# A gated mix of attention and a long convolution: operand layout, load sizes, a fourth buffer and a re-planned order

## The chip, the cores and the metric

The kernel runs on one core of a Trainium2 chip. The metric is the time of one execution on the device in microseconds, where lower is better. Three executions of the kernel before took 659.38, 667.66 and 668.18 us, so the median is 667.66 us. One further execution was profiled.

A core has engines that run side by side and synchronise by semaphores. TensorE (PE in the profile) multiplies matrices: a weight load (PEld) puts one operand into the array, and a matmul streams the other past it into PSUM. VectorE (DVE) and ScalarE (ACT) work element by element. GpSimd (POOL) makes constants here. SyncE (SP) issues nearly all transfers (DMA). Each engine takes its instructions strictly in the order written.

## What is computed

The inputs are one sequence `x` of 2048 positions with 448 channels, and the parameters of two branches. In short:

```python
g = sigmoid((x * gate_w).sum(-1, keepdims=True))
# a: 16 query heads of 28 channels, one key and one value head
q = x @ wq; k = x @ wk; v = x @ wv
p = softmax(q k^T * 28**-0.5)              # per head, 2048 x 2048
a = (p @ v) @ wo
# b: one causal convolution of length 2048 per channel
dt = exp(log_dt)
K[d, l] = Re(sum_n C[d,n] * exp(dt[d] * A[d,n] * l) * dt[d] * B[d,n])   # 256 complex n
b[:, d] = causal_convolution(x[:, d], K[d]) + x[:, d] * Dskip[d]
return g * a + (1 - g) * b
```

## The kernel before

**Attention.** `prep_x` transposes `x` into `xT` (channels on partitions) with TensorE and copies the result out of PSUM, half with ScalarE (L490) and half with VectorE (L492). It then makes keys (L498), values and the gate (L514). `qproj` (L649 to L661) makes the queries of four heads for 512 positions. `main` walks through 1024 tiles of scores, 128 keys by 512 queries each, in sets of three and two tiles by turns: the scores (L973, four heads in four row strips of the array), one exponential per set on ScalarE (L986), and, two sets later, the product with the values (L995, four heads in four column strips). Sixteen times an accumulator is finished; `norm` (L895 to L904) then moves the denominators through DRAM with nine transfers. `outp` multiplies with `wo` and `fold` adds the result into `O`.

**Convolution.** For each group of 32 channels VectorE builds tables of powers (`masters`, then `tables`, L744 to L781) in `tab`, and from them TensorE makes the kernel's values (`kgen`, L799), 16 channels per call, which go to the DRAM scratch `KP`. From there `tload` brings four channels as a Toeplitz operand of 1 MB into one of three slots of `T` (L824). `conv` (L841) multiplies it with `U`, a copy of `x` cut into pieces of 64 positions: for each slot there are 8 steps, each of them four matmuls, one per channel, side by side in four column strips. The weights are a column of `U` with one element every 448 (896 bytes), 32, 30, and so on down to 18 of them; the moving operand is 128 elements of `T` with one in four. A second product (L861) and an addition (L869) put the result into `O`.

**Where things lie.** Early data share memory with later data: `x` is staged in `tab`, the six parameter arrays in `O`, their products in `T`, `tmp` and `tab`, `wq` in `mbf`, and `wk` in `rho`. `consts` clears or fills buffers, some with long memsets on GpSimd: `Wq` with 2048 elements per partition, `Wo` with 1792, the second half of `U` with 7168. `prep_params` later clears `O` with 7168 (L632).

**What sets the order.** `Prog` collects the operations with their reads, writes, an assumed duration and a priority `pr` (a low number goes first). `schedule` is a planner at build time: it simulates the engines with the assumed durations and always takes the operation that can start earliest, among equals the one with the lowest `pr`. Scores have 0, values 0.5, kgen 1.7, the convolution 4. The order that results is fixed, and the semaphore waits are worked out from it (`emit`). A transfer is assumed to cost its issuing queue 60 ns, then a time for its bytes on one shared DMA resource, then 2200 ns (`DMA_NS`). The semaphore latency and extra slack are constants too. PSUM bank `psX` is shared by several steps under a lock.

Of the kernel before, what the change touches and what calls it, by code (L numbers as in the profile page):

```python
# [11 lines left out]
P = 128  # L12
# [18 lines left out]
NTR = 3  # L31
# [25 lines left out]
class Op:  # L57
    __slots__ = ("i", "eng", "fn", "ns", "lat", "deps", "pr", "lock", "unlock", "slot", "ndma",
                 "count", "vc", "end", "comm")


class Prog:
# [44 lines left out]
    def dma(self, pairs, desc, slot, rd=(), wr=(), pr=0, eng="sp", slow=False):  # L107
# [6 lines left out]
        o.slot, o.ndma = slot, len(pairs)  # L114
# [6 lines left out]
    def schedule(self):  # L121
# [19 lines left out]
        while done < n:  # L141
# [155 lines left out]
class Kernel:  # L297
# [25 lines left out]
    def alloc(self):  # L323
# [25 lines left out]
        self.U = sb("U", 32 * D, BF)  # L349
# [3 lines left out]
        self.rho = sb("rho", 32 * 64, BF)  # L353
        self.tmp = sb("tmp", 2 * 16 * EW, BF)
# [16 lines left out]
    def consts(self):  # L371
        pg = self.pg
        V = lambda b, off, n: b.v(0, P, off, [[1, n]])
        pm = lambda ap, val, ns, key, pr=0: pg.op("pool", lambda e: e.memset(ap, val), ns, wr=key, pr=pr)
        pm(V(self.ident, 0, P), 1.0, 200, ["id"])
# [3 lines left out]
        sm = self.small  # L379
        pm(V(self.Wq, 0, NT * 512), 0.0, 1500, ["Wq"])  # L380
        pg.op("dve", lambda e: e.tensor_reduce(V(sm, 0, 1), self.ident.v(0, P, 28, [[32, 4]]), AX.X, ALU.max),
              100, rd=["id"], wr=["s0"])
        pg.op("dve", lambda e: e.memset(V(sm, 1, 1), 0.5 * math.pi), 60, wr=["hpi"])
        pg.op("dve", lambda e: e.memset(V(self.Wk, 0, NT * P), 0.0), 300, wr=["Wk"])
        pm(V(self.Wm, 0, P), 0.0, 100, ["Wm"], 1)
        for hb in range(4):
            pm(self.Wm.v(32 * hb, 28, 32 * hb + 28, [[1, 1]]), -1.0, 60, ["Wm"], 1)
        pg.op("dve", lambda e: e.memset(self.vaug.v(0, P, 28, [[32, 16]]), 1.0), 80, wr=["va"])
        pg.op("dve", lambda e: e.memset(self.vaug.v(0, P, 29, [[32, 16], [1, 3]]), 0.0), 80, wr=["va"])
# [11 lines left out]
        pg.op("dve", lambda e: e.memset(V(self.kstg, 0, 256), 0.0), 100, wr=[("kst", 0)], pr=3)  # L401
        pm(V(self.skt, 0, D // 4), 0.0, 100, ["skt"], 4)
        pm(V(self.Wo, 0, NT * D), 0.0, 1500, ["Wo"], 4)
        pm(V(self.U, 16 * D, 16 * D), 0.0, 6000, ["U"], 5)

    def loads(self):
# [7 lines left out]
        raw = self.O  # L414
# [662 lines left out]
```

## Time and profile before

| what | value |
|---|---|
| median of three runs | 667.66 us (659.38 to 668.18) |
| the profiled execution's own time | 664.46 us |
| its span, first to last instruction | 662.7 us |
| mean granted TensorE clock | 0.828 |
| TensorE matmul busy | 553.9 us, 84% of the span |
| ScalarE busy | 498.3 us, 75% |
| VectorE busy | 475.7 us, 72% |
| GpSimd busy | 19.3 us, 3% |
| first exponential (L986) starts | 30.95 us |
| moved by transfers | 133.46 MB, mean 201 GB/s |

A row of a group reads: line, engine, operation, what it writes `<-` what it reads, shape, `x` count, then the busy time in us, the mean duration of one in ns, and the idle time just before these instructions with what ended it. A row of waits reads: engine, line and tile that waited, `<-` the engine and line that released it, total us, times, longest. A row of a timeline gives the start in us, the duration in us, the engine and the line; neighbouring instructions of one line are merged with their count, so a merged duration includes the run-out of the last one. Ends of matmuls are modelled, and a matmul that waits inside the array counts as busy.

### The profile page before, as it was taken

How to read it: one execution, taken by the hardware profiler on the slowest of the kernel's cores; microseconds unless marked ns; L12 is line 12 of the kernel's file. 1: busy time of each engine (PE TensorE's matmuls, PEld its weight loads, DVE VectorE, ACT ScalarE, POOL GpSimd, SP SyncE). 2: the span in 40 equal slices, each digit the busy share in tenths (PEclk: the TensorE clock that was granted, in tenths of full speed). 3: DMA queues.
4: the chain of work that ended last, by engine and by line, in shares of the span. 5: the costliest groups of instructions: out<-in, count | busy, mean ns of one | idle time of the engine just before them, and what ended most of it. 6: DMA issues, size and time to landing. Idle time of an engine off the chain costs nothing.

```text
span 662.7 us, 18405 instructions
## 1 busy us (share of the span) xinstructions
PE 553.9 (84%) x8234; PEld 269.0 (41%) x8234; DVE 475.7 (72%) x1045; ACT 498.3 (75%) x427; POOL 19.3 (3%) x24
## 2 busy tenths in 40 slices
PE   3787688999698988897889888988999987877775
PEld 2422132546354544453446345544554433311112
DVE  6679999898979999889797889989997221110002
ACT  3578778788778886886886787877888886779891
POOL 8003000000000000000000000000000000000000
PEclk9955557989899998899798998988988996855556
DMA  9630018787857678578778786878479669530000
GB/s 189 155 81 0 5 26 281 246 320 212 325 194 270 210 277 310 206 239 286 280 244 286 257 279 227 301 253 305 129 266 315 195 208 324 207 100 1 17 1 28
DMA packets 41262, 133.46 MB, mean 201 GB/s; under 512 B 10352, under 2 KB 24928, under 8 KB 26848
## 3 DMA queue, kind: packets, MB, share of 16 engines
q1 hardware_dynamic: 41184, 132.30, 59.9%
q8 instruction: 64, 1.05, 0.6%
q14 instruction: 14, 0.11, 0.0%
HBM read 128.31 MB, written 3.85 MB: 199 GB/s over the span
## 4 chain that ended last, share of the span: by engine, by line
PE 37%; DMA 29%; DVE 17%; ACT 12%; SPq 3%; issue 1%; DVEq 0%
DMA T<-KP_scratch 18%; ACT expT L986 12%; PE psS L973 9%; PE psS L841 8%; PE psX L799 6%; PE psB L995 6%; DMA denT<-acc 5%; SPq L111 3%; PE psX L649 2%; DVE tab L760 2%; DMA R_scratch<-denT 2%; DVE tmp L761 2%; DMA rdenB<-R_scratch 2%; DVE qT L661 1%; PE psX L878 1%; DVE acc L895 1%
## 5 line engine op out<-in xcount | busy, mean ns | idle before, releaser
L986 ACT ACTIVATE expT<-psS 128x1536 bf16<-128x1536 f32 (+1 forms) x410 | 483.5, 1255 | 134.4 <-PE psB L995 84.8
L973 PE MATMUL psS<-qT,kT 29*128 29x512 bf16 x1024 | 189.4, 458 | 43.2 <-ACT expT L986 42.1
L841 PE MATMUL psS<-T,U 128*32 128x128 bf16 (+7 forms) x3584 | 156.8, 307 | 31.7 <-DMA T<-KP_scratch 28.1
L841 PEld LDWEIGHTS psS<-T,U 128*32 128x32 bf16 (+7 forms) x3584 | 107.7, 155 | 77.8 <-DMA T<-KP_scratch 37.1
L995 PE MATMUL psB<-expT,vaug 128*32 128x512 bf16 x1024 | 111.7, 464 | 1.7 <-DVE acc L895 1.7
L973 PEld LDWEIGHTS psS<-qT,kT 29*128 29x128 bf16 x1024 | 40.5, 94 | 159.2 <-ACT expT L986 108.9
L799 PE MATMUL psX<-tab 128*32 128x64 bf16 x1792 | 78.7, 330 | 3.5 <-DVE kstg L812 1.7
L760 DVE TENSOR_TENSOR tab<-tab,mbf 128x4096 bf16<-128x4096 bf16 (+4 forms) x70 | 69.6, 995 | 0.0
L761 DVE TENSOR_TENSOR tmp<-tab,mbf 128x256 bf16<-128x256 bf16 (+4 forms) x70 | 69.2, 989 | 0.0
L799 PEld LDWEIGHTS psX<-tab 128*32 128x32 bf16 x1792 | 62.3, 155 | 16.3 <-issue 6.9
L995 PEld LDWEIGHTS psB<-expT,vaug 128*32 128x32 bf16 x1024 | 22.8, 97 | 64.0 <-issue 59.2
L895 DVE COPY acc<-psB 128x512 f32<-128x512 f32 x16 | 11.1, 692 | 44.8 <-PE psB L995 44.7
L763 DVE TENSOR_TENSOR tab<-tab,tmp 128x128 bf16<-128x128 bf16 (+4 forms) x70 | 39.9, 569 | 0.0
L850 DVE TENSOR_TENSOR cst<-psS,omq 128x512 bf16<-128x512 f32 x28 | 19.2, 686 | 28.5 <-PE psS L841 28.3
L765 DVE TENSOR_TENSOR tab<-tab,tmp 128x128 bf16<-128x128 bf16 (+4 forms) x70 | 39.7, 567 | 0.0
L776 DVE TENSOR_TENSOR tab<-tab,rho 128x4096 bf16<-128x4096 bf16 x14 | 32.0, 2288 | 0.0
L649 PE MATMUL psX<-xT,Wq 112*128 112x512 bf16 x64 | 22.5, 451 | 5.8 <-DVE Wq L440 5.8
L684 DVE TENSOR_TENSOR msq<-mst 128x256 f32<-128x256 f32 x63 | 27.1, 430 | 0.0
L904 DVE TENSOR_TENSOR onT<-acc,rdenB 128x512 bf16<-128x512 f32 x15 | 10.5, 702 | 22.8 <-DMA rdenB<-R_scratch 22.8
L772 DVE TENSOR_TENSOR rho<-rho,mbf 128x64 bf16<-128x64 bf16 (+4 forms) x70 | 25.4, 363 | 0.0
L900 DVE RECIPROCAL denT<-denT 128x16 f32<-128x16 f32 x15 | 3.8, 254 | 23.4 <-DMA denT<-acc 23.4
L869 DVE TENSOR_TENSOR O<-O,psX 128x256 bf16<-128x256 bf16 x28 | 11.6, 416 | 12.4 <-PE psX L861 12.3
(109 smaller groups left out, 351.0 us busy)
## 6 DMA issues: line engine op xcount, KB each, us to landing
T<-KP_scratch SPq DMA_DIRECT2D x112, 1024.0 KB, 7.2
rdenB<-R_scratch SPq DMA_DIRECT2D x60, 64.0 KB, 2.2
tab<-in_A_x_dram SPq DMA_DIRECT2D x4, 448.0 KB, 9.4
U<-in_A_x_dram SPq DMA_DIRECT2D x16, 112.0 KB, 3.0
KP_scratch<-kstg SPq DMA_DIRECT2D x28, 64.0 KB
out_dram<-O SPq DMA_DIRECT2D x3, 448.0 KB, 3.8
denT<-acc SPq DMA_DIRECT2D x60, 2.0 KB, 2.7
U<-in_A_x_dram SPq DMA_DIRECT2D x16, 56.0 KB, 2.2
```

Source lines behind the costliest of these rows:

```text
L649: pg.op("pe", lambda e, T=T: e.matmul(px, self.Wq.v(0, DT, T * 512 + g * 128, [[1, 128]]), self.xT.v(0, DT, T * S + 512 * qc, [[1, 512]]), ...
L684: pg.op("dve", lambda e, k=k: e.tensor_tensor(msq.v(0, P, 0, [[BW, 2], [1, BW]]), both(k - 1), both(k - 1), ALU.mult), el(2 * BW), rd=keys ...
L760: vo(lambda e, dst=dst, src=src, mr=mr: e.tensor_tensor(dst, src, mr, ALU.mult), 2 * n, done + mk(lv), [kr, ki])
L761: vo(lambda e, src=src, mi=mi, w=w: e.tensor_tensor(tmp.v(0, P, 0, [[w * EW, 2], [EW, w], [1, EW]]), src, mi, ALU.mult), 2 * n, done + mk( ...
L763: vo(lambda e, do=do, n=n: e.tensor_tensor(tab.v(0, P, do, [[1, n]]), tab.v(0, P, do, [[1, n]]), tmp.v(0, P, n, [[1, n]]), ALU.subtract), ...
L765: vo(lambda e, do=do, n=n: e.tensor_tensor(tab.v(0, P, do + BLK, [[1, n]]), tab.v(0, P, do + BLK, [[1, n]]), tmp.v(0, P, 0, [[1, n]]), ALU ...
L776: vo(lambda e: e.tensor_tensor(tab.v(0, P, FM, [[64, 2], [EW, 32], [1, 64]]), tab.v(0, P, lo + 31 * EW, [[BLK, 2], [-EW, 32], [1, 64]]), r ...
L799: r = e.matmul(self.psX.v(32 * g, 32, 64 * jj, [[1, 64]]), tab.v(0, P, lo + comp * BLK + 64 + o, [[EW, 32]]), tab.v(0, P, fo, [[mo - fo, 2 ...
L841: r = e.matmul(ps.v(32 * j, 32 - 2 * n, po + 128 * k, [[1, 128]]), self.U.v(0, P, 2 * n * D + 4 * gi + j, [[D, 32 - 2 * n]]), self.T.v(0, ...
L973: r = e.matmul(self.psS.v(0, P, 512 * (bo + k), [[1, 512]]), kT.v(32 * h, DH + 1, 128 * kt, [[1, 128]]), qT.v(32 * h, DH + 1, 512 * (i % 2 ...
L986: pg.op("act", lambda e: e.activation(expT.v(0, P, 512 * es, [[1, n]]), self.psS.v(0, P, 512 * bo, [[1, n]]), AF.Exp, scale=SQ), 130 + n / ...
L995: r = e.matmul(self.psB.v(32 * h, 32, 0, [[1, 512]]), vaug.v(0, P, 32 * kt, [[1, 32]]), expT.v(0, P, 512 * (t % 10), [[1, 512]]), start=(k ...
```

## The change

- `U` is stored as 448 channels times 32 pieces instead of 32 times 448, so the weights of a convolution step lie side by side. The loads can no longer write that order directly. They go to two staging halves in `tab` (behind the staged `x`), which VectorE clears first, and 16 copies on GpSimd reorder them into `U`.
- `T` gets a fourth slot. To make room, `rho` shares memory with `tmp`, `tmp` is halved, and the last doubling step of a table uses the `Fm` area of `tab` for its product. The parameter arrays are staged in `T`, their products in `T` and `mbf`.
- `x`, the projection weights and the parameters are loaded in rows of up to 3584 bytes, with four neighbouring positions or channels on one partition. The steps that read them undo the permutation by their strides (L490, L492 and the transposes). Three weight loads and `log_dt` are issued from ScalarE's queue.
- The clearing of `Wq` (now only its gaps), `Wo` and `O` moves to VectorE, that of half of `U` is gone.
- The planner's figures change: 300 ns on the queue per transfer, 3000 ns more until a `T` load lands, 310 instead of 215 ns for half a kgen column, 250 instead of 330 ns for a value product, 260 instead of 240 ns for an output product, and for an exponential 100 ns plus its elements with a latency of 130 ns (130 and 60 before).

```diff
-NTR = 3
+NTR = 4
-    def dma(self, pairs, desc, slot, rd=(), wr=(), pr=0, eng="sp", slow=False):
+    def dma(self, pairs, desc, slot, rd=(), wr=(), pr=0, eng="sp", slow=False, extra=0):
...
-                free[e] = r + 60.0 * o.ndma
+                free[e] = r + 300.0 * o.ndma
...
-                end = dmafree + self.DMA_NS
+                end = dmafree + self.DMA_NS + o.extra
...
-        self.U = sb("U", 32 * D, BF)
+        self.U = sb("U", D * 32, BF)
...
-        self.rho = sb("rho", 32 * 64, BF)
-        self.tmp = sb("tmp", 2 * 16 * EW, BF)
+        self.tmp = sb("tmp", 2 * 8 * EW, BF)
+        self.rho = self.tmp
...
-        pm(V(self.Wq, 0, NT * 512), 0.0, 1500, ["Wq"])
+        dm(self.Wq.v(0, P, 28, [[32, 64], [1, 4]]), 0.0, 300, ["Wq"])
...
+        for k in range(2):
+            dm(V(self.tab, self.stg + k * 8 * D, 8 * D), 0.0, 1500, [("ust", k)])
...
-        pm(V(self.Wo, 0, NT * D), 0.0, 1500, ["Wo"], 4)
-        pm(V(self.U, 16 * D, 16 * D), 0.0, 6000, ["U"], 5)
+        dm(V(self.Wo, 0, NT * D), 0.0, 810, ["Wo"], 5)
+        for q in range(4):
+            dm(V(self.O, q * 4 * D, 4 * D), 0.0, 800, [("O", q)], 5)
...
-            pg.dma([(self.xst.v(0, P, q * 4 * D, [[D, 4], [1, D]]), dram(x, q * 4 * P * D, [[D, P], [P * D, 4], [1, D]]))],
-                   (512, 896), f"x{q}", wr=[("xst", q)])
+            pg.dma([(self.xst.v(0, P, q * 4 * D, [[1, 4 * D]]), dram(x, q * 4 * P * D, [[4 * D, P], [1, 4 * D]]))],
+                   (128, 3584), f"x{q}", wr=[("xst", q)])
...
+            pg.dma(lst, (1024 if k < 2 else 512, 896), f"u{k}", wr=[("ust", k % 2)], pr=0.5)
+            for j in range(0, 8, 2):
+                pg.op("pool", lambda e, k=k, j=j: e.tensor_copy(
+                    self.U.v(0, P, 8 * k + j, [[32, D], [1, 2]]),
+                    self.tab.v(0, P, self.stg + (k % 2) * 8 * D + j * D, [[1, D], [D, 2]])), 1500,
+                    rd=[("ust", k % 2)], wr=[("U", k), "ustd"], pr=1)
...
-        pg.op("pool", lambda e: e.memset(self.O.v(0, P, 0, [[1, 16 * D]]), 0.0), 6000, rd=["rawdone"],
-              wr=["raw0"] + [("O", q) for q in range(4)], pr=6)
...
-            vo(lambda e, src=src, mi=mi, w=w: e.tensor_tensor(tmp.v(0, P, 0, [[w * EW, 2], [EW, w], [1, EW]]), src, mi, ALU.mult),
-               2 * n, done + mk(lv), ["tmp"])
+            tb, to, tk = (tmp, 0, "tmp") if lv < 4 else (tab, FM, "Fm")
...
-                pg.op("pe", lambda e, mm=mm, comp=comp: mm(e, comp), 215, rd=keys, wr=[X, ("kst", ks)], pr=1.7,
+                pg.op("pe", lambda e, mm=mm, comp=comp: mm(e, comp), 310, rd=keys, wr=[X, ("kst", ks)], pr=1.7,
...
-               (128, 8192), f"T{s}", rd=[("KP", gi // 4), "pad"], wr=w, pr=1)
+               (128, 8192), f"T{s}", rd=[("KP", gi // 4), "pad"], wr=w, pr=1, extra=3000)
...
-                                     self.U.v(0, P, 2 * n * D + 4 * gi + j, [[D, 32 - 2 * n]]),
+                                     self.U.v(0, P, (4 * gi + j) * 32 + 2 * n, [[1, 32 - 2 * n]]),
...
-                                                AF.Exp, scale=SQ), 130 + n / 1.2, rd=bk, wr=[("e", t % 10) for t in ts], pr=0)
+                                                AF.Exp, scale=SQ), 100 + n / 1.2, rd=bk, wr=[("e", t % 10) for t in ts], pr=0, lat=130)
...
-            pg.op("pe", mm, 330, rd=["va"] + [("e", t % 10) for t in ts], wr=[("b", 6)], pr=0.5)
+            pg.op("pe", mm, 250, rd=["va"] + [("e", t % 10) for t in ts], wr=[("b", 6)], pr=0.5)
```

More of the change, by code (lines that the diff above doesn't have):

```diff
@@ L58 @@
     __slots__ = ("i", "eng", "fn", "ns", "lat", "deps", "pr", "lock", "unlock", "slot", "ndma",
-                 "count", "vc", "end", "comm")
+                 "count", "vc", "end", "comm", "extra")
 class Prog:
@@ L436, in loads @@
-        for k in range(1, 6):
-            lraw(k)
+        lraw(1)
         pg.op("dve", lambda e: e.tensor_copy(self.Wk.v(0, DT, 0, [[32, 16], [1, DH]]),
```

140 lines of the change are left out of this document (75 added, 65 removed).

## The prediction

> **What bounds the kernel now.** First ScalarE's slices on the page and the busy times by stage (the row is: stretch, length, busy time of each engine, granted clock, DMA share), to see which engine is full where; then the waits, to see what the fuller engine stands for; then the order of single instructions around one such wait.
>
> ```profile
> ACT  3578778788778886886886787877888886779891
> ...
> core 0: us, PE busy (x) PEld busy (x) DVE busy (x) ACT busy (x) POOL busy (x), PEclk, DMA share, GB/s
> 0.00:31.00 31.00, 17.11 (x162) 11.96 (x162) 20.75 (x31) 13.10 (x15) 13.26 (x23) 1.00 0.85 184
> 31.00:100.00 69.00, 53.86 (x401) 17.04 (x400) 60.94 (x157) 53.25 (x47) 6.07 (x1) 0.51 0.12 29
> 100.00:586.00 486.00, 429.83 (x7399) 227.80 (x7396) 386.45 (x845) 376.78 (x318) 0.00 (x0) 0.91 0.74 254
> 586.00:650.00 64.00, 47.54 (x253) 8.81 (x253) 2.75 (x6) 55.16 (x49) 0.00 (x0) 0.50 0.10 30
> 650.00:663.00 13.00, 5.58 (x27) 3.36 (x23) 4.80 (x8) 0.00 (x0) 0.00 (x0) 0.61 0.11 35
> ```
>
> ScalarE's slices are full only near the end. There are five stages: a front of 31 us before the first exponential, attention alone, the long stage with the convolution (100 to 586 us), attention alone again, and the tail. In 586:650, without convolution, 49 exponential sets take 64 us, 1.31 us each, and ScalarE is busy for 55.16 of them: it is the bound there. In 100:586 the 318 sets take 1.53 us each, and ScalarE stands still for 486 - 376.78 = 109 us. TensorE is busy for 429.83 of 486 (88%) and takes its instructions in the written order. So the long stage goes at the pace of TensorE's queue, with VectorE (386.45, 80%) close behind. Who waits there:
>
> ```profile
> PEld psS L973 <- ACT expT L986: 108.9, 176, 2.0
> ACT expT L986 <- PE psB L995: 84.8, 55, 3.4
> ACT expT L986 <- PE psS L973: 47.5, 72, 3.7
> PEld psS L841 <- DMA T<-KP_scratch: 37.1, 32, 3.9
> PE psS L841 <- DMA T<-KP_scratch: 28.1, 24, 3.6
> PE psX L649 <- DVE Wq L440: 5.8, 1, 5.8
> PE psS L498 <- DVE Wk L438: 2.2, 1, 2.2
> ```
>
> The convolution (L841) is the one place in the long stage where TensorE waits on a transfer: 28.1 us as matmul, 37.1 us as weight load, in 32 waits. ScalarE's largest wait is for L995 (probabilities times values). One of these places, TensorE, SyncE and ScalarE:
>
> ```profile
> 165.59 0.62 PE L995 MATMUL psB<-expT,vaug 128*32 128x512 bf16 x8
> 168.31 0.98 PE L841 MATMUL psS<-T,U 128*32 128x128 bf16 x24 [2.11 <-DMA T<-KP_scratch]
> ...
> 160.48 0.58 SPq L111 DMA_DIRECT2D T<-KP_scratch  x1
> ...
> 179.76 2.37 ACT L986 ACTIVATE expT<-psS 128x1024 bf16<-128x1024 f32 x2 [2.18 <-PE psB L995]
> ...
> T<-KP_scratch SPq DMA_DIRECT2D x112, 1024.0 KB, 7.2
> ```
>
> The load issued at 160.48 was written in as if it landed sooner; TensorE stood 2.11 us at it with the next scores queued behind, and a like stall shortly after leaves ScalarE idle for 2.18 us. The planner's own figure for such a load is 128 x (105 + 0.022 x 8192) / 16 x 1.1 = 2.5 us, plus DMA_NS 2.2, together 4.7 us; the median row says 7.2.
>
> **The change, part by part.**
>
> *T loads.* With `extra=3000` the plan expects 7.7 us, above the median of 7.2, and the fourth slot lets a load start one use earlier. What is late next is a load far above the median, or one held on SyncE. I take 80% of the 37.1 us: -30. Bounds: -37.1, and 0 if the stalls only change their place. The plan also charges 300 ns per issue on SyncE where it charged 60, and 0.58 is the row: better, still short. What lies on that queue behind a T load is the normalisation's nine issues per head.
>
> *U contiguous in time.* Only the weight load of L841 reads U; the moving operand T keeps its step of four elements.
>
> ```profile
> L841 PE MATMUL psS<-T,U 128*32 128x128 bf16 x448 | 38.4, 327 | 31.7 <-DMA T<-KP_scratch 28.1 <-DVE cst L850 2.9
> L841 PE MATMUL psS<-T,U 128*30 128x128 bf16 x448 | 36.6, 309 | 0.0
> L841 PE MATMUL psS<-T,U 128*18 128x128 bf16 x448 | 35.3, 300 | 0.0
> L841 PEld LDWEIGHTS psS<-T,U 128*30 128x30 bf16 x448 | 22.6, 185 | 4.0 <-issue 3.5
> L841 PEld LDWEIGHTS psS<-T,U 128*18 128x18 bf16 x448 | 16.5, 132 | 4.8 <-issue 4.4
> ...
> 111.59 0.15 PEld L841 LDWEIGHTS psS<-T,U 128*24 128x24 bf16 x4
> 111.81 0.28 PE L841 MATMUL psS<-T,U 128*24 128x128 bf16 x4
> ...
> 159.74 0.92 PE L841 MATMUL psS<-T,U 128*24 128x128 bf16 x24
> 162.06 1.33 PE L841 MATMUL psS<-T,U 128*28 128x128 bf16 x36
> ```
>
> Nine groups of four in 1.33 us and six in 0.92 give 0.137 us per group. From 30 weight columns to 18 the load falls by 53 ns and the matmul by 9 only, so inside a burst the weights do not set the pace. Where the weights had been loaded 0.22 us ahead (111.59 against 111.81) the group still took 0.28 us: that is the time with the load wholly hidden. Against it the 32-column form, mostly the first of a burst, takes 0.327, so 0.047 x 112 = 5.3 us is exposed; if every group lost what the mean of 307 ns shows over 280, it would be 896 x 0.027 = 24 us. I take -9, nearer the low end because groups overlap in a burst. A cost below nothing, a slower contiguous load, has no row for it: 0 is the other end.
>
> A rule speaks for more. The Trainium skill, "SBUF — State Buffer", section "Door 1: The DMA port swizzle", says that consecutive reads of one 16-byte line go at full rate and each crossing to a new line pays: T at 8 bytes would be free and U at 896 bytes the culprit. By it the sum would be the one of the second rival below, 575 in place of 619. The trace speaks against it, by the nearly constant matmul row.
>
> *Front.* The GpSimd memsets go to VectorE or shrink.
>
> ```profile
> 0.95 0.27 DVE L384 MEMSET Wk<- 128x256 uint32 x1
> 7.11 1.53 DVE L438 COPY Wk<-rho 112x448 bf16<-112x448 bf16 x1
> 8.56 0.38 DVE L578 CAST cst<-acc 128x448 bf16<-128x448 f32 x1
> 8.97 6.22 DVE L579 TENSOR_SCALAR rdenB<-cst 128x448 f32<-128x448 bf16 x1
> 56.23 5.17 DVE L727 CAST mbf<-qst 128x128 bf16<-128x128 f32 x1
> ...
> 2.94 0.29 POOL L376 TENSOR_SCALAR_AFFINE_SELECT ident<-ident 128x128 bf16<-128x128 bf16 x1
> 8.57 6.38 POOL L374 MEMSET U<- 128x7168 bf16 x1
> 55.25 6.07 POOL L632 MEMSET O<- 128x7168 bf16 x1 [40.30 <-PE psX L588]
> ...
> U<-in_A_x_dram SPq DMA_DIRECT2D x16, 112.0 KB, 3.0
> tab<-in_A_x_dram SPq DMA_DIRECT2D x4, 448.0 KB, 9.4
> ```
>
> L579 ends with the U memset (15.19 against 14.95), a like operation takes 0.38; so 5.8 us go there, about 1.1 in L438 and 5.0 in L727: 12 us of VectorE. On the path to the first exponential stand TensorE's 5.8 us for Wq and 2.2 for Wk, 8.0 together. Added on VectorE: memsets of 2 x 3584, 4 x 1792 and 1792 elements, by the 0.27 us for 512 elements 8.5 us; the first two are issued at the start, where VectorE is otherwise idle, and if that cover is gone the 3.8 us of them delay the first xT copy. Copying xT out in another order may cost the four L492 copies their double rate. GpSimd gets 16 copies of 896 elements. No copy of that engine is in the trace: by the memset row (0.89 ns an element) 0.8 us, by the affine select (2.3 ns) 2.1 us, so 13 to 33 us in all. A staging load lands some 3 us after its issue (the U row), behind the x pieces (the tab row), so they start at about 10 to 14 us and have until the first convolution, after 100 us: that covers them. VectorE can be held by them as it was by the memset; the whole 33 us is the upper end of that cost, 0 the lower, and I take 8, since a hold lasts one copy.
>
> Those copies add a wait: the loads u0 and u1 reuse the staging halves, so SyncE waits at them for GpSimd, and the parameters and Wo queue behind; and the opening memset of table 1 (VectorE, L637) waits for all 16. Their 32 issues stay as they were, earlier in the queue. The weight loads moved to ScalarE's queue cost five issues there while it has nothing to do. Longer pieces for x can bring its landing (9.4 us) forward by some us or not; I count nothing, it is what is late next. So: 8.0 gained on the first exponential, VectorE's table chain at -12 + 8.5 + 8 = +4.5, of which part is covered by the earlier start; net -6, bounds -12 and +10.
>
> *New order of buffers.* Part of the tables' products now uses the Fm area and rho the tmp area, so table c's last quarter waits for the kgen before it. In the trace VectorE never waits for that reader, and 15 us of table work lie ahead of it; 0, with up to 14 x 1 us if TensorE runs late.
>
> Sum: 664.46 (the profiled execution, 1.76 over its span of 662.7) - 30 - 9 - 6 = 619.5, so **619 us**. The median of the three runs is 667.66; I take the sum without adding that 3 us.
>
> **The rivals.** *First, a wider gain.* With the stalls gone the order fits and ScalarE's other stalls shrink too. VectorE then ends the tables: 386.45 us of work in the long stage at 95% busy is 407, plus about 20 us for the last convolutions, 427 instead of 486. 664 - 59 - 6 - 9 = 590. For it: ScalarE waits 132 us in all for TensorE, far more than T explains. Against it: VectorE waits too. Chance 0.12.
>
> *Second, the weights did set the pace.* Then a group falls to TensorE's rate for contiguous reads. In the stall above two groups of L995 with 512 columns took 0.62 us, the run-out of the last included: at most 0.31 each, 0.078 for 128 columns. 896 x (0.137 - 0.078) = 53 us off TensorE in place of 9: 664 - 53 - 30 - 6 = 575, or the 590 above as far as VectorE holds it. Against it: the matmul rows by weight columns. Chance 0.05.
>
> *Third, the T stalls stay*, moved by SyncE's queue or by DMA time: 112 loads in 450 us instead of 486 lift the DMA share from 0.74 to 0.80. Then only -9 and -6, with a few us of T: 645. Chance 0.16.
>
> *Fourth, nothing moves*: the front's cost at its upper end eats the rest, 655 to 667. Chance 0.08.
>
> *Fifth, slower: an order written for a faster TensorE.*
>
> ```profile
> L995 PE MATMUL psB<-expT,vaug 128*32 128x512 bf16 x1024 | 111.7, 464 | 1.7 <-DVE acc L895 1.7
> L799 PE MATMUL psX<-tab 128*32 128x64 bf16 x1792 | 78.7, 330 | 3.5 <-DVE kstg L812 1.7 <-DVE tab L781 1.4 <-DVE qT L661 0.3
> ```
>
> L995 is now planned at 250 ns per group (330 before); by its row it holds TensorE for 436. 111.7 / 256 = 0.436, so 256 x 0.186 = 48 us of TensorE time are not in the plan. kgen, by contrast, goes from 215 to 310 ns, its 224 groups of eight by the row at 351: 30 us unplanned become 9. But L995 stands right ahead of ScalarE's next set (the 84.8 us), kgen does not. If all 48 us come back as stalls, and the T loads still cost half of their 30, 619 + 48 + 15 = 682. It decides if ScalarE's wait for L995 rises from 84.8 above some 130 us. Chance 0.08.
>
> **The numbers.** My forecast has 0.51, its own range 600 to 640. Within 2% of 667.66 (654.3 to 681.0) is about what a measurement of this kernel, whose three runs span 9 us, cannot tell from no change. Faster: 0.51 + 0.12 + 0.05 and 0.13 of the third, 0.81. Same: 0.03 + 0.08 = 0.11. Slower 0.08. The range reaches to 582, leaving out the second rival, and up to 658, leaving out the slower one and part of the fourth: some 0.17 outside.
>
> **What would show it.** The waits of L841 for T fall under 10 us (else the third rival); ScalarE's idle time in the long stage falls from 109 to near 75; the L841 matmuls stay near 300 ns while their weight loads fall toward 100 (matmuls near 220 mean the second rival); the first exponential starts near 23 us and no VectorE instruction there takes 5; the long stage lasts near 447 us; the last stages keep 64 and 13 us. The prediction is wrong if TensorE is as full as before and the stage no shorter, or if GpSimd's copies run up to the first convolution.

## The result, and the profile after

The kernel after took 636.98 us (median of 4 runs, 633.82 to 639.88) against 667.92 us for the kernel before beside it: a ratio of 0.9558, 95% interval 0.9481 to 0.9636, so it is faster. Its profiled execution took 636.67 us with a span of 635.0 us, against 664.46 and 662.7. The forecast was 619, its range 582 to 658: the sign was right, the size too large: 45 us expected, 28 measured on the profiled executions.

The busy share of ScalarE and of the DMA engines in 40 slices, from the page of the kernel after, and its busy time by stage (columns as in the prediction):

```profile
ACT  3689797988879878796968989787889678879740
...
DMA  9510000666916727686957576864768360798993
```

```profile
0.00:28.50 28.50, 16.65 (x162) 11.75 (x162) 24.61 (x42) 13.34 (x15) 13.48 (x28) 0.91 0.71 207
28.50:121.00 92.50, 74.46 (x521) 21.63 (x524) 71.34 (x154) 77.97 (x68) 8.25 (x8) 0.56 0.13 37
121.00:611.00 490.00, 426.76 (x7348) 205.77 (x7341) 375.15 (x848) 403.46 (x345) 0.00 (x0) 0.91 0.68 244
611.00:635.00 24.00, 11.99 (x213) 7.63 (x211) 6.84 (x12) 0.38 (x1) 0.00 (x0) 0.77 0.54 196
```

The five stages have become four. The second stage of attention alone, 64 us before, is gone: the convolution now starts at 121 us (103 before) and its last matmul starts at 623.5 (577.7), after the last exponential, which ends at 611.4 (649.0). The tail after the last exponential has grown from 13.7 to 23.6 us and is no longer attention: TensorE still works through 213 instructions there, and the DMA engines are 54% busy, after four slices at 80% or more. The end of the chain of waits says who sets the end now (start, duration, what it is):

```profile
614.44 8.23 DMA T<-KP_scratch
622.67 0.04 issue
622.71 1.14 PE psS L856 x27
```

The chain stands 8.23 us on a `T` load for the last convolution, and all that follows waits for that. It is the last of 24 `T` loads that are issued from 538.2 us on, behind a pause of 20.4 us in which SyncE's queue stands 16.8 us for a convolution (L856) that has still to read its slot. The 24 loads land by 622.7 us, one every 3.5 us. The waits of the kernel after, in the form of those shown before:

```profile
ACT expT L1001 <- PE psB L1010: 68.2, 54, 5.2
...
ACT expT L1001 <- PE psS L988: 33.1, 52, 2.5
...
PEld psS L856 <- DMA T<-KP_scratch: 8.9, 6, 3.1
...
PE psS L856 <- DMA T<-KP_scratch: 7.1, 6, 2.8
...
PE psX L672 <- DVE Wb L538: 4.7, 1, 4.7
```

The waits for `T` did fall, from 32 to 6, as the prediction said. ScalarE's waits for TensorE fell too, from 132.3 to 101.3 us. The time can be accounted for on ScalarE alone, since the 410 exponentials run one behind the other. The start of the first came 2.4 us earlier, the exponentials themselves take 3.3 us less, the gaps between them 31.9 us less (134.6 to 102.7, summed over the trace), and the tail 9.9 us more: 2.4 + 3.3 + 31.9 - 9.9 = 27.7 us, which is the difference of the spans. Of the 31.9 us, 19.2 lie between the first and the last convolution matmul (105.7 us of gaps over 311 exponentials before, 86.5 over 344 after: 0.25 us a gap in place of 0.34), 11.2 went with the second stage of attention alone, and 1.5 lie ahead of the convolution. The granted clock of the long stage is 0.91 in both kernels, so the clock does not explain what closed there. So what has to be found is what closed the gaps, and what brought the tail.

### The profile page after: what moved, and what is told of

Its sections match the earlier page's. It is cut to its first block, busy times and chain, and to the rows that moved or that the text cites. A ratio compares the mean times of both kernels' runs of the same rounds, so it can differ in the third digit from the quotient of the medians.

```text
span 635.0 us, 18423 instructions
## 1 busy us (share of the span) xinstructions
PE 529.9 (83%) x8234; PEld 246.8 (39%) x8234; DVE 478.0 (75%) x1055; ACT 495.1 (78%) x427; POOL 21.7 (3%) x36
## 4 chain that ended last, share of the span: by engine, by line
DVE 43%; PE 22%; DMA 20%; ACT 9%; SPq 4%; issue 1%; ACTq 0%
ACT expT L1001 8%; DVE tab L774 7%; PE psS L988 6%; DMA denT<-acc 6%; DMA T<-KP_scratch 5%; DMA R_scratch<-denT 4%; DMA rdenB<-R_scratch 4%; PE psB L1010 4%; SPq L111 4%; PE psS L856 3%; DVE tmp L776 3%; PE psX L814 3%; DVE tab L778 3%; DVE tab L776 3%; DVE tab L780 3%; DVE tab L791 2%
## 5 line engine op out<-in xcount | busy, mean ns | idle before, releaser
L1001 ACT ACTIVATE expT<-psS 128x1536 bf16<-128x1536 f32 (+1 forms) x410 | 480.1, 1256 | 103.1 <-PE psB L1010 68.2
L988 PE MATMUL psS<-qT,kT 29*128 29x512 bf16 x1024 | 182.9, 441 | 44.5 <-ACT expT L1001 41.5
L856 PE MATMUL psS<-T,U 128*32 128x128 bf16 (+7 forms) x3584 | 143.0, 292 | 21.9 <-DVE cst L865 14.6
L856 PEld LDWEIGHTS psS<-T,U 128*32 128x32 bf16 (+7 forms) x3584 | 89.9, 106 | 64.0 <-issue 28.1
L1010 PE MATMUL psB<-expT,vaug 128*32 128x512 bf16 x1024 | 109.8, 455 | 0.1
L814 PE MATMUL psX<-tab 128*32 128x64 bf16 x1792 | 84.7, 332 | 7.1 <-DVE kstg L827 4.6
L1010 PEld LDWEIGHTS psB<-expT,vaug 128*32 128x32 bf16 x1024 | 22.8, 96 | 60.1 <-issue 57.4
L776 DVE TENSOR_TENSOR tmp<-tab,mbf 128x256 bf16<-128x256 bf16 (+3 forms) x56 | 37.5, 669 | 0.0
L791 DVE TENSOR_TENSOR tab<-tab,tmp 128x4096 bf16<-128x4096 bf16 x14 | 32.0, 2283 | 0.1
L776 DVE TENSOR_TENSOR tab<-tab,mbf 128x4096 bf16<-128x4096 bf16 x14 | 31.9, 2279 | 0.0
L919 DVE TENSOR_TENSOR onT<-acc,rdenB 128x512 bf16<-128x512 f32 x15 | 10.3, 689 | 27.7 <-DMA rdenB<-R_scratch 27.7
L824 DVE CAST kstg<-psX 128x256 bf16<-128x256 f32 x28 | 11.8, 420 | 20.4 <-PE psX L814 20.4
L787 DVE TENSOR_TENSOR tmp<-tmp,mbf 128x64 bf16<-128x64 bf16 (+4 forms) x70 | 25.1, 359 | 0.6
L778 DVE TENSOR_TENSOR tab<-tab,tmp 128x128 bf16<-128x128 bf16 (+3 forms) x56 | 23.4, 417 | 0.4
L780 DVE TENSOR_TENSOR tab<-tab,tmp 128x128 bf16<-128x128 bf16 (+3 forms) x56 | 22.9, 409 | 0.0
```

What stands on the lines that cost most here:

```text
L776: vo(lambda e, src=src, mi=mi, w=w, tb=tb, to=to: e.tensor_tensor(tb.v(0, P, to, [[w * EW, 2], [EW, w], [1, EW]]), src, mi, ALU.mult), 2 * ...
L778: vo(lambda e, do=do, n=n, tb=tb, to=to: e.tensor_tensor(tab.v(0, P, do, [[1, n]]), tab.v(0, P, do, [[1, n]]), tb.v(0, P, to + n, [[1, n]] ...
L780: vo(lambda e, do=do, n=n, tb=tb, to=to: e.tensor_tensor(tab.v(0, P, do + BLK, [[1, n]]), tab.v(0, P, do + BLK, [[1, n]]), tb.v(0, P, to, ...
L791: vo(lambda e: e.tensor_tensor(tab.v(0, P, FM, [[64, 2], [EW, 32], [1, 64]]), tab.v(0, P, lo + 31 * EW, [[BLK, 2], [-EW, 32], [1, 64]]), r ...
L814: r = e.matmul(self.psX.v(32 * g, 32, 64 * jj, [[1, 64]]), tab.v(0, P, lo + comp * BLK + 64 + o, [[EW, 32]]), tab.v(0, P, fo, [[mo - fo, 2 ...
L856: r = e.matmul(ps.v(32 * j, 32 - 2 * n, po + 128 * k, [[1, 128]]), self.U.v(0, P, (4 * gi + j) * 32 + 2 * n, [[1, 32 - 2 * n]]), self.T.v( ...
```

## The experiments

Twelve kernels were run. One number serves in several of them: the time in which only one of the two streams is at work, that is, the distance between the end of the last exponential and the start of the last convolution matmul.

### Which operand sets the pace of a convolution step

`u_step` takes only the layout of `U` back, in the same written order:

```diff
-                                     self.U.v(0, P, (4 * gi + j) * 32 + 2 * n, [[1, 32 - 2 * n]]),
+                                     self.U.v(0, P, 2 * n * D + 4 * gi + j, [[D, 32 - 2 * n]]),
```

> The kernel after, with one edit: the weights of the convolution are again read with one element every 448 (from the new array, so other values of x enter and the convolution's sums are other numbers). The order of all instructions is that of the kernel after. Theory 1 (the weights are not the pace of a burst): groups of four go back from 0.116 us to about 0.122, the first of a burst pays some 0.05 us, together 5 to 10 us of TensorE; time 637 + 3 to + 8, that is 640 to 645. Rival (the contiguous weights carry the gain): time near that of the kernel before, 660 or more.

It took 643.04 us, ratio 0.9683 (0.9636 to 0.973), as the first theory has it. Two of its groups by form, and after them the same of the kernel after:

```profile
L856 PE MATMUL psS<-T,U 128*32 128x128 bf16 x448 | 37.7, 321 | 20.5 <-DVE cst L865 15.1 <-DMA T<-KP_scratch 4.9 <-DVE absq L669 0.5
L856 PE MATMUL psS<-T,U 128*30 128x128 bf16 x448 | 36.4, 308 | 0.5 <-issue 0.5
```

```profile
L856 PE MATMUL psS<-T,U 128*30 128x128 bf16 x448 | 34.3, 294 | 0.0
...
L856 PE MATMUL psS<-T,U 128*18 128x128 bf16 x448 | 34.4, 293 | 0.0
...
L856 PE MATMUL psS<-T,U 128*32 128x128 bf16 x448 | 33.5, 287 | 21.9 <-DVE cst L865 14.6 <-DMA T<-KP_scratch 7.1
...
L856 PEld LDWEIGHTS psS<-T,U 128*30 128x30 bf16 x448 | 13.2, 106 | 4.7 <-issue 3.4
...
L856 PEld LDWEIGHTS psS<-T,U 128*18 128x18 bf16 x448 | 13.0, 103 | 4.3 <-issue 3.2
```

With the weights side by side their load takes 103 to 106 ns whatever the columns (132 to 185 before), and the matmul loses its dependence on them: 294 ns with 30 columns, 293 with 18. The layout is worth some 6 us by the medians, 8 by the ratios.

`t_close` reads the moving operand as 128 neighbouring elements (so it multiplies with the wrong elements of `T`; the work is the same in number and shape):

```diff
-                                     self.T.v(0, P, s * 4096 + (896 - 128 * n) * 4 + j, [[4, 128]]),
+                                     self.T.v(0, P, s * 4096 + (896 - 128 * n) * 4 + 128 * j, [[1, 128]]),
```

> The kernel after, with one edit: the moving operand of the convolution is read as 128 neighbouring elements, not one in four (so wrong elements of the Toeplitz operand enter). The order is that of the kernel after. Theory 1 (the step of the moving operand sets the pace): a group of four takes 0.055 to 0.065 us where it took 0.116, its matmul row falls from 292 ns to about 225, some 45 us of TensorE time; the end falls less, to 605 to 625, because VectorE's tables (busy 478 us) and the loads at the end stay. Rival (four matmuls with their weight loads cost 0.116 us whatever they read): row and time stay at 292 ns and 637.

A burst of eight groups in the timeline, first of the kernel after, then of `t_close`, both at full clock (the first but for its first group); then the span and the granted clock of `t_close` and its clock in slices; and last the scores and the value products, of the kernel after and of `t_close`:

```profile
299.73 1.11 PE L856 MATMUL psS<-T,U 128*26 128x128 bf16 x32
```

```profile
305.63 0.63 PE L856 MATMUL psS<-T,U 128*26 128x128 bf16 x32
```

```profile
core 0: 646.3 us, clock 0.730
```

```profile
PEclk8755558786579867767779978777986765976566
```

```profile
L988 PE MATMUL psS<-qT,kT 29*128 29x512 bf16 x1024 | 182.9, 441 | 44.5 <-ACT expT L1001 41.5 <-DVE qT L675 1.3 <-DMA T<-KP_scratch 0.2
L1010 PE MATMUL psB<-expT,vaug 128*32 128x512 bf16 x1024 | 109.8, 455 | 0.1
```

```profile
L988 PE MATMUL psS<-qT,kT 29*128 29x512 bf16 x1024 | 202.4, 489 | 60.3 <-ACT expT L1001 50.5 <-DVE qT L675 6.2 <-DVE tab L778 0.6
L1010 PE MATMUL psB<-expT,vaug 128*32 128x512 bf16 x1024 | 123.0, 509 | 0.5 <-DVE acc L910 0.4
```

The burst takes 0.63 in place of 1.11 us. By the starts of successive groups, a group at full clock takes 0.056 us in place of 0.116 (medians). So the step of four elements in the moving operand does set the pace there. But the kernel did not gain, and the first theory's 605 to 625 us was missed: it took 649.15 us, ratio 0.9773 (0.9727 to 0.9819), 12 us slower than the kernel after. The mean granted clock fell from 0.854 to 0.730. Nearly half of the successive groups now run at half clock, and there a group takes 0.107 us; in the kernel after it takes 0.116 at half clock and at full clock alike. So the step costs much only where the clock is full. The scores and the value products, which the edit does not touch, keep TensorE busy for 33 us more, and the convolution for 29.5 us less (143.0 to 113.5). The order of the instructions is the same in both, so the loss comes with the clock; why the clock is granted less was not tried.

### The planner's figures and the fourth slot

`plan_old` is the kernel after with the six old figures of the planner (three of them in the diff), `before_plan` the kernel before with the six new ones:

```diff
-                free[e] = r + 300.0 * o.ndma
+                free[e] = r + 60.0 * o.ndma
...
-               (128, 8192), f"T{s}", rd=[("KP", gi // 4), "pad"], wr=w, pr=1, extra=3000)
+               (128, 8192), f"T{s}", rd=[("KP", gi // 4), "pad"], wr=w, pr=1)
...
-            pg.op("pe", mm, 250, rd=["va"] + [("e", t % 10) for t in ts], wr=[("b", 6)], pr=0.5)
+            pg.op("pe", mm, 330, rd=["va"] + [("e", t % 10) for t in ts], wr=[("b", 6)], pr=0.5)
```

> The kernel after with the six planner figures of the kernel before (60 ns per issue, no 3000 ns for T, kgen 215, value product 330, output product 240, exponential 130 with latency 60). Buffers, layouts and loads are those of the kernel after. Theory 1 (the planner's T latency carries most of the gain): waits of the convolution for T go back from 8.9 to over 25 us and the time to 655 to 665. Rival (buffers, layout and front carry it): waits stay under 15 us, time 632 to 645.

> The kernel before with the six new planner figures alone (and one dependency at the last convolution step that the new order needs); three T slots, old layout, old loads, long GpSimd memsets. Theory 1: most of the gain is here, 635 to 650, waits for T under 15 us against 37.1. Rival (the fourth slot or the layout is needed): 655 to 670.

`plan_old` took 654.0 us (0.9843, 0.9794 to 0.9891) and `before_plan` 662.95 us (0.9957, 0.9915 to 0.9999). So the figures bring 17 us with the new buffers and about 3 with the old ones. The waits for `T` in `plan_old` are back at 31.1 us as weight load, as the first theory had it, and its time is 1 us under that theory's range; in `before_plan` they are halved (37.1 to 17.7 us) and the time hardly moves. In `before_plan` the streams have changed places: the last exponential ends at 619.5, the last convolution matmul starts at 647.4.

`slots3` is the kernel after with three slots, planned anew:

```diff
-NTR = 4
+NTR = 3
...
-        self.T = sb("T", NTR * 4096, BF)
+        self.T = sb("T", 4 * 4096, BF)
```

> The kernel after with three T slots used in place of four (memory laid out as in the kernel after, order planned anew). Theory 1 (the plan's T latency removes the stalls, the fourth slot only lets loads run further ahead): 637 to 645. Rival (a load now held three times as long by the plan needs the fourth slot, as the 663 us of the three-slot kernel with the new figures suggests): 648 to 660, and the last convolution ends more than 15 us after the last exponential.

It took 667.88 us, ratio 1.0005 (0.9962 to 1.0049): all of the gain is gone, more than either theory expected. Its waits for `T`, and its last stages:

```profile
PEld psS L856 <- DMA T<-KP_scratch: 31.5, 20, 3.7
...
PE psS L856 <- DMA T<-KP_scratch: 31.3, 20, 3.4
```

```profile
121.00:601.00 480.00, 414.42 (x6928) 195.62 (x6937) 372.92 (x843) 401.54 (x345) 0.00 (x0) 0.90 0.66 224
601.00:650.00 49.00, 24.36 (x605) 17.40 (x603) 7.83 (x16) 0.34 (x1) 0.00 (x0) 0.67 0.82 302
```

Attention ends earlier than in any other kernel here, at 601.3 us, and then the convolution alone needs 48 us more, with TensorE half idle and the DMA engines 82% busy. Attention had been given TensorE's time, and three slots could not make up for it.

`slots4_alone` is the reverse, the kernel before with only a fourth slot (and the sharing of memory that it needs), and `slots4_plan` adds the six figures to that:

```diff
-NTR = 3
+NTR = 4
...
-        self.rho = sb("rho", 32 * 64, BF)
-        self.tmp = sb("tmp", 2 * 16 * EW, BF)
+        self.tmp = sb("tmp", 2 * 8 * EW, BF)
+        self.rho = self.tmp
...
-                6: (fM, 0), 7: (fM, W2), 8: (fF, FO), 9: (fF, FO + W2)}
+                6: (fT, 6 * W2), 7: (fT, 7 * W2), 8: (fF, FO), 9: (fF, FO + W2)}
...
+            tb, to, tk = (tmp, 0, "tmp") if lv < 4 else (tab, FM, "Fm")
```

> The kernel before with a fourth T slot and nothing else of the change but what makes room for it (rho shares tmp, the last table level's products pass through the Fm region, two prologue scratches move into T); planner figures, layout of U, loads and memsets as before. Planned again, its order ends the convolution early, as before's does (13th pair of convolutions at the 850th QK tile, before: 855). Theory 1 (two streams: the later of attention and convolution sets the end; a slot helps only where the convolution is the late one): T waits of TensorE fall from 32 and 28 us to under 15, last exp still near 640, conv ends near 575, time 652 to 668. Theory 2 (the slot carries the gain by itself, since its loss cost 31 us in the kernel after): 632 to 645.

> The kernel before with the fourth T slot and the six planner figures of the change, with U's old layout, the old loads and the long GpSimd memsets. Theory 1 (slot and figures together are the gain; the layout of U is worth 6 us and the new front little): 638 to 650, last exp and last convolution within 20 us of each other, under 625 both. Theory 2 (the front and the layout carry more than the single runs show, or the figures only fit the new order): 652 or more.

`slots4_alone` took 667.04 us (0.9977, 0.9924 to 1.003), `slots4_plan` 640.25 us (0.961, 0.9542 to 0.9677). The waits for `T` and the stage of attention alone in `slots4_alone`, and then the waits for `T` in `slots4_plan`:

```profile
PEld psS L842 <- DMA T<-KP_scratch: 30.3, 33, 3.0
...
PE psS L842 <- DMA T<-KP_scratch: 20.5, 22, 2.5
```

```profile
574.00:650.00 76.00, 56.73 (x320) 10.68 (x316) 5.77 (x10) 65.04 (x57) 0.00 (x0) 0.52 0.08 26
```

```profile
PE psS L842 <- DMA T<-KP_scratch: 6.6, 5, 2.0
PEld psS L842 <- DMA T<-KP_scratch: 6.3, 6, 2.3
```

A slot by itself changes nothing: the written order still ends the convolution at 574 us and leaves 57 exponential sets behind it. That its `T` waits stay above 20 us, where theory 1 had them under 15, was a miss: without the 3000 ns the plan still places the matmuls ahead of the landings. Slot and figures together, with the old layout, the old loads and the long memsets, give nearly the whole result, as theory 1 had it. The table puts the seven kernels side by side. The times are medians, each ratio is to runs of the kernel before made beside it, and the columns behind the ratio are from the profiled execution, in us; the gaps are those between exponentials, the tail is what follows the last one:

| kernel | slots | figures | us | ratio to before | last exponential ends | last convolution matmul starts | one stream alone | gaps | tail |
|---|---|---|---|---|---|---|---|---|---|
| before | 3 | old | 667.92 | 1 | 649.0 | 577.7 | 71 | 134.6 | 13.7 |
| `slots4_alone` | 4 | old | 667.04 | 0.9977 | 650.0 | 573.8 | 76 | 136.8 | 13.4 |
| `before_plan` | 3 | new | 662.95 | 0.9957 | 619.5 | 647.4 | 28 | 109.3 | 39.3 |
| `slots4_plan` | 4 | new | 640.25 | 0.9610 | 625.3 | 611.0 | 14 | 114.9 | 13.7 |
| `plan_old` | 4 | old | 654.0 | 0.9843 | 636.1 | 584.5 | 52 | 125.7 | 13.4 |
| `slots3` | 3 | new | 667.88 | 1.0005 | 601.3 | 649.6 | 48 | 94.4 | 59.7 |
| after | 4 | new | 636.98 | 0.9558 | 611.4 | 623.5 | 12 | 102.7 | 23.6 |

(The first four have the old layout, loads and memsets, the last three the new ones.) The two kernels in which the streams end close together are the fast ones. The last two columns say how. The new figures close the gaps with either number of slots: 134.6 to 109.3 us with three, 136.8 to 114.9 with four, and 125.7 to 102.7 with the new layout. With three slots the late convolution takes this back as a tail of 39.3 or 59.7 us; with four the tail is 13.7 or 23.6. With the old figures the tail is short already, so a slot finds nothing to shorten.

### Is a wait for T worth its length

`extra0` takes the 3000 ns out of the plan, `extra1000` puts 1000 in their place (the diff is that of `extra0`):

```diff
-               (128, 8192), f"T{s}", rd=[("KP", gi // 4), "pad"], wr=w, pr=1, extra=3000)
+               (128, 8192), f"T{s}", rd=[("KP", gi // 4), "pad"], wr=w, pr=1)
```

> The kernel after with one planner figure back: no 3000 ns more for a T load (order planned anew). Theory 1: the convolution's waits for T rise from 8.9 to over 20 us and the time to 643 to 655. Rival (the other five figures made the 17 us that all six are worth): waits may rise, time 632 to 641.

> The kernel after with 1000 instead of 3000 ns of extra planned load time. In the planned order of TensorE the convolution is spread more evenly (steps of 37 to 90 QK tiles between pairs of convolutions, after: 45 to 97) and its 13th pair stands at tile 950 instead of 1010. Theory 1 (the later stream sets the end): last exp 615 to 622, last convolution 605 to 618, the time after the last exp back to about 14 to 16 us, 628 to 634. Theory 2 (TensorE's work fixes the end, and spreading it changes nothing): within 2 us of the kernel after, 635 to 639, whichever stream ends last. T waits 15 to 30 us in both.

The waits for `T` in `extra0`:

```profile
PEld psS L856 <- DMA T<-KP_scratch: 32.8, 32, 2.5
PE psS L856 <- DMA T<-KP_scratch: 23.6, 26, 2.2
```

The 32 waits are back at nearly their old length, and `extra0` takes 636.46 us (0.9541, 0.9491 to 0.9591), as the kernel after does. It has 12.8 us more gaps between exponentials and 11.5 us less tail; its streams end 4 us apart (625.2 and 621.4). Since the order is another one too, the runs do not show how much of the 12.8 us is the stalls' doing. `extra1000` ends its convolution at 601.7, its exponentials at 622.0, and takes 638.08 us (0.9581, 0.9512 to 0.965), the tail at 13.3 us, with waits for `T` of 22.0 us as weight load. That is the second theory's time, not the first's: with some 20 us between the ends, an even spreading is worth nothing more here.

### The figure for the value product, and the one for kgen

`pv330` plans the value product at 330 ns, as before, and leaves the rest of the kernel after:

```diff
-            pg.op("pe", mm, 250, rd=["va"] + [("e", t % 10) for t in ts], wr=[("b", 6)], pr=0.5)
+            pg.op("pe", mm, 330, rd=["va"] + [("e", t % 10) for t in ts], wr=[("b", 6)], pr=0.5)
```

> The kernel after with one planner figure back: 330 ns for a value product, not 250 (order planned anew; the trace of the kernel after has 109.8 us for 256 products, 429 ns). Fifth rival of the prediction (250 makes ScalarE wait for this product): ScalarE's wait for it falls from 68.2 us by 10 or more, time 620 to 630. Theory 1 (it hardly matters, TensorE's queue is full either way): 633 to 643.

It took 654.95 us (0.9803, 0.9752 to 0.9854), which neither theory expected. Its `T` loads on SyncE's queue in the stretch where its DMA engines go quiet, and ScalarE's wait for the product:

```profile
495.26 0.51 SPq L111 DMA_DIRECT2D T<-KP_scratch  x1
499.47 16.77 SPq L111 DMA_DIRECT2D KP_scratch<-kstg  x2
...
540.29 0.58 SPq L111 DMA_DIRECT2D KP_scratch<-kstg  x1
```

```profile
ACT expT L1001 <- PE psB L1010: 83.4, 54, 5.1
```

For 53.8 us no `T` load is issued, and for 35.9 of them SyncE's queue waits for `kstg`, the kernel values that the loads need (L827); 28 of the 112 then remain, and the convolution ends at 642.2, over 90 us later. In the kernel after the longest such pause this late is the 20.4 us above, with 24 loads behind it. Was it then the figure of 250 that made the difference? `kgen_only` has the five other old figures, 330 among them, and keeps only kgen's new 310 ns (the diff is against `plan_old`):

```diff
-                pg.op("pe", lambda e, mm=mm, comp=comp: mm(e, comp), 215, rd=keys, wr=[X, ("kst", ks)], pr=1.7,
+                pg.op("pe", lambda e, mm=mm, comp=comp: mm(e, comp), 310, rd=keys, wr=[X, ("kst", ks)], pr=1.7,
```

> The kernel after with five of the six old planner figures; the sixth, the planned time of a kernel-generation group on TensorE, stays at the new 310 ns (old: 215). In the planned order the 13th pair of convolutions then stands at the 940th QK tile, where the kernel with all six old figures has it at 893, extra1000 at 950, extra0 at 980 and the kernel after at 1010. Theory 1 (what counts is how far into the attention the order spreads the convolution, and any figure that puts its end near tiles 940 to 1010 gives the gain): 635 to 643, last exp 620 to 630, last convolution 595 to 622. Theory 2 (the gain comes from the value product's figure of 250 ns, which this kernel lacks, as its run with 330 alone lost 18 us): 650 to 658, last exp above 632.

It took 643.37 us, ratio 0.9711 (0.9582 to 0.9841), the last exponential at 625.3, the last convolution matmul at 597.5. The time lies just above the first theory's range and clearly below the second's: without the 250, one figure that moves the convolution later in the order gives by the medians about 11 of the 17 us that all six give. By the ratios it is 9 of 19, with an interval too wide to tell the share. So the 3000 ns need not be there, and a good part of the gain comes without the 250; what counts is the order that comes out, and a change of one figure can give a poor one, as in `pv330`.

### GpSimd's copies

`pool_short` cuts the 16 copies into `U` to 1/28 of their length and fills `U` by plain loads (so the convolution's weights are not the right ones), in the same written order of the other engines:

```diff
-                    self.U.v(0, P, 8 * k + j, [[32, D], [1, 2]]),
-                    self.tab.v(0, P, self.stg + (k % 2) * 8 * D + j * D, [[1, D], [D, 2]])), 1500,
+                    self.U.v(0, P, 8 * k + j, [[32, 16], [1, 2]]),
+                    self.tab.v(0, P, self.stg + (k % 2) * 8 * D + j * D, [[1, 16], [D, 2]])), 1500,
```

> The kernel after with the 16 GpSimd copies cut to one twenty-eighth of their elements; U is filled instead by two plain loads of x (so the convolution's operand holds wrong values). Order as in the kernel after, but for these two loads on SyncE. If GpSimd's copies hold VectorE in the front: VectorE's operations there that took 0.96, 1.80 and 1.32 us take 0.6, 1.1 and 1.1, the first exponential starts 1 to 3 us earlier than 28.5. Theory 1 (this is a small part of the late start of the convolution, the rest is order): the convolution starts 0 to 4 us earlier than 121.0, time 632 to 638. Rival (the copies cause the late start): it starts near 105, time 615 to 625.

It took 634.34 us (0.9499, 0.9443 to 0.9555), no measurable difference from the kernel after. The front of the kernel after, GpSimd and VectorE, and then the same VectorE instructions in `pool_short`:

```profile
17.60 10.44 POOL L464 COPY U<-tab 128x896 bf16<-128x896 bf16 x8 [12.60 <-DMA tab<-in_A_x_dram]
...
19.24 0.96 DVE L619 TENSOR_SCALAR T<-T 128x896 f32<-128x896 f32 x1
...
20.24 1.80 DVE L620 SCALAR_TENSOR_TENSOR T<-T 128x896 f32<-128x896 f32 x1
...
25.24 0.67 DVE L538 TENSOR_SCALAR Wb<-Wm,small 128x128 bf16<-128x128 bf16 x1
```

```profile
21.77 0.62 DVE L619 TENSOR_SCALAR T<-T 128x896 f32<-128x896 f32 x1
...
22.42 1.09 DVE L620 SCALAR_TENSOR_TENSOR T<-T 128x896 f32<-128x896 f32 x1
...
26.47 0.25 DVE L538 TENSOR_SCALAR Wb<-Wm,small 128x128 bf16<-128x128 bf16 x1
```

The copies do hold VectorE up, by 0.3 to 0.7 us an instruction, but with them cut short the first exponential still starts at 29.4 us, where 1 to 3 us less than 28.5 was expected, and the convolution at 121.5. The rival (the copies cause the late start) is out, with 634 us in place of 615 to 625.

## Why the prediction was right, and where it was wrong

**Sign and range** held: the time is 637, between 582 and 658. The sum was 17 us low on the profiled execution. That the time lies in the range is in part luck: the largest term of the sum is not what shortened the run, and the gain came by a path that the prediction does not have. Of its signs, the waits for `T`, the matmuls of L841 near 300 ns and their weight loads near 100 came as said; those on the long stage did not. The stage was to last near 447 us and lasts 490; ScalarE's idle time in it was to fall to near 75 us and is 86.5 (490 - 403.46). "TensorE is as full as before and the stage no shorter", its sign of being wrong, is what came: TensorE is busy for 87% of 490 us, against 88% of 486. What changed is that the stage holds 345 exponential sets in place of 318, 1.42 us each in place of 1.53.

**The step that failed is "I take 80% of the 37.1 us: -30".** Its first half came true: the waits of L841 for `T` (now L856) fell under 10 us. Its second half, that the run gets shorter by 80% of that wait, did not. In `extra0` the stalls are back and the time is the same, and in `extra1000` more than half of their length is (22.0 us as weight load); in `before_plan` they are halved and the time moves by 3 us. In `slots4_alone` and `slots3` stalls and lost gain go together, and in `plan_old` a third of the gain is there in spite of them (31.1 us of waits as weight load), of which the layout of `U` can make 6 to 8 us.

What carried the gain in place of the stalls is the written order together with the slot. The new figures end the convolution later among the exponentials: none of the 410 sets starts after the last convolution matmul (52 before). In the old layout the new figures leave 0 with three slots and 9 with four; the old figures leave 39 in `plan_old` and 57 in `slots4_alone`. That the convolution also starts later, behind 66 sets in place of 47, does not come from the figures: it is 64 in `plan_old` and 53 in `slots4_plan`. The gaps between exponentials shrink by 31.9 us, and the convolution becomes the late stream, which a fourth slot lets keep up. The prediction had named the 3000 ns first; by `extra0` the kernel is as fast without them.

**"The last stages keep 64 and 13 us" was the plain error that goes with it.** The stage of attention alone could not stay as long as the convolution's place in the order moved, and the tail could not stay at 13 when the convolution came to end last. The prediction read each stage by the row that ends last within it, and never asked when each of the two streams ends; the 64 us with VectorE busy for 2.75 of them were the sign that the order was lopsided.

**U contiguous, -9:** measured 6 to 8, and the reason was right: the weights do not set the pace in a burst. The 0.137 us per group that the prediction took from two merged rows is 0.124 by the starts of successive groups (median), 0.123 in `u_step` and 0.116 in the kernel after. `u_step` and `t_close` settle the second rival (the weights set it). By the Trainium skill, "SBUF — State Buffer", section "Door 1: The DMA port swizzle", a step of 8 bytes would read at full rate; here it reads at 0.116 us a group where neighbouring elements take 0.056 at full clock, so the trace disagrees.

**Front, -6, the first exponential near 23 us:** it came at 28.53, 2.4 us earlier in place of 8. TensorE's 5.8 and 2.2 us for `Wq` and `Wk` are gone, but it now waits 4.7 us for `Wb` (L538), which VectorE reaches only at 25.24, behind 4 us of parameter work (L619 to L622) that the order puts ahead of it. The four copies of `xT` that the prediction named and did not price went from 0.69 to 1.16 us each (L492, now L510). "No VectorE instruction takes 5 us" held, "8" for GpSimd's hold was too much: the three rows above add 1.5 us. That the net of the front is about nothing agrees with `slots4_plan`, which lacks it and the layout of `U`, is 3 us slower than the kernel after, and has an interval that overlaps its.

**The rivals.** The first, a wider gain (590), named the right wait, ScalarE's 132 us for TensorE, which fell by 31, but not the tail. The third had the `T` stalls stay and the time at 645; `extra0` shows that they can stay at 636. The fourth, the front's cost eating the rest, did not come. The fifth, an order written for a faster TensorE, is refuted in its mechanism: ScalarE's wait for L995 (now L1010) fell from 84.8 to 68.2 us, and giving the plan 330 again raised it to 83.4 and the time by 18 us, in an order that differs in more than this wait.

**What stays open:** which property of the order closes the gaps. One stream alone for under 30 us goes with 634 to 649 us in eight kernels, over 45 us with 654 to 668 in four; but `before_plan` (28 us alone, 663) and `pv330` (16 us alone, 655) lie off this line, the first with a tail of 39.3 us at three slots, the second with its pause in the loads. So the distance of the ends is a sign and no proof. The traces say where the gaps closed (19.2 of the 31.9 us between the first and the last convolution matmul), but no run changes the order alone in one place to show why they close. The clock's drop in `t_close` was not tried either.

## What to carry to other kernels

Where two streams share an engine, find first when each of them ends, and price a change by what it does to the later one: the length of a wait does not say what its removal is worth. Here 32 waits could come back without any change of the time. Parts that do nothing alone can be the whole gain together, so an ablation from both ends (one part added to the old kernel, one part taken from the new) tells more than either. When a planner's figures change, compare the order that comes out before any cost: the place of the last convolution among the exponential sets, with the gaps and the tail that go with it, told more here than the length of any wait.

## What the runs showed of the hardware

- At full granted clock a moving operand with a step of four bf16 elements goes through the array at half the pace: 0.116 us for four matmuls of 128 columns side by side, 0.056 us with neighbouring elements. At half clock the two take 0.116 and 0.107 us.
- With these matmuls made shorter and the order kept, the mean granted clock was 0.730 in place of 0.854 (0.730 to 0.775 in four runs, against 0.845 to 0.857), and the kernel took 12 us longer.
- A GpSimd copy of 896 bf16 elements takes about 1.1 to 1.3 us (4.31 us for four, 10.44 for eight), and a VectorE operation with two SBUF operands beside it 1.80 in place of 1.09 us. The Trainium skill, "SBUF — State Buffer", section "Who interferes with whom", has such an operation contend with a GpSimd instruction that reads SBUF; these rows agree.
